# A fused attention and MLP kernel on one core: new load order, new order of the first MLP units, casts moved between engines, last output product by token block

## The chip, the core and the metric

The kernel runs on one core of one Trainium2 chip. The time is the device time of one execution in microseconds (us); the span of the profile is about 1.8 us shorter. PE is the matmul engine (TensorE), PEld its weight load, DVE is VectorE, ACT is ScalarE, POOL is GpSimd, SP is SyncE, which here only issues DMAs. "Granted clock" is the share of full speed that the profile says PE was given. "Unit (c, j)" below means the j-th of the 16 slices of 128 hidden columns of the MLP for chunk c of 512 tokens; there are nine chunks.

## The reference, cut to what matters

```
q_s = softmax(q, axis=-1)                 # 8 batches, 8 heads, 576 tokens, 64 wide
k_s = softmax(k, axis=2)                  # over the tokens
kv  = einsum('bhsd,bhse->bhde', k_s, v)
x   = einsum('bhsd,bhde->bhse', q_s, kv)  # heads joined: 4608 tokens x 512
h   = x @ w_in                            # 512 -> 2048
out = (h * sigmoid(beta * h)) @ w_out     # 2048 -> 512, float32
```

## The kernel before

One chunk is the first 512 tokens of one batch; the ninth chunk collects the 64 left-over tokens of all eight. For each unit the kernel does `mm_a` (four matmuls, then tanh on ACT and a product on DVE, which give `g`), and two units later `mm_b` (four matmuls that add `g` times a slice of `w_out` into four accumulators). In the code cuts NJ is these 16 slices, LAG the two units, HP the four head pairs, and `warm(n)` issues n dummy matmuls whose result nobody reads. All inputs are float32, so weights, `v`, `k` and `q` pass through a cast or an exponential before PE can use them. While chunk c runs, `side` prepares batch c + 1. Chunks 0 and 1 are special, because they run while the weights still arrive. I call the stretch from the end of chunk 0's units to chunk 1's unit 4 the bridge.

The loads and the start of chunk 0:

```python
load_q(0, parts=2)
nc.sync.dma_start(beta_r[:], ...)
load_kv(k_st, k, 0, "k_st", parts=2)
w_load("in", 0, 0)                       # half of the first block of w_in
load_kv(v_st, v, 0, "v_st", parts=4)
w_load("in", 0, 1)
w_load("out", 0); w_load("in", 1); w_load("out", 1); w_load("in", 2)
w_load("out", 2); w_load("in", 3)
load_q(1, parts=2); w_load("out", 3)
load_kv(k_st, k, 1, ...); load_kv(v_st, v, 1, ...)
# ... cut: memsets, identities ...
warm(18)                                 # dummy matmuls
# ... cut: exponential, sum and product of q ...
for s in range(2):
    for j in (2 * s, 2 * s + 1):
        q_pet(0, j, nc.scalar if s == 0 else nc.vector)   # transpose on PE, copy
    warm(10 if s == 0 else 2)
for j in range(HP):
    kz_exp(0, j)                         # two exponentials on ACT each
# ... for each of four head pairs: cast v, kv product, normalise,
#     x product (copied by ACT), mm_a of units 0 and 1, one quarter each
```

Then units 2 to 15 of chunk 0, `mm_a(0, u)` and `mm_b(0, u - 2)` in turn, with the weight casts and the q work of batch 1 between them; the bridge; and the tail:

```python
for s in range(2):
    vz_cast(1, 2 * s, nc.vector, m=2)
for jj in range(2):
    kv_mm(1, jj); kv_norm(1, jj)
mm_b(0, NJ - 2)
for j in range(HP):
    x_mm(1, j, ...)
# ... mm_a of units (1, 0) and (1, 1) ...
finish_b(0, NJ - 1)                      # last mm_b of chunk 0 and its stores
# ... cut: seven equal chunks ...
for st, j in ((0, J0), (0, J1), (1, J0), ...):    # last three units, mixed
    mm_b(B, j, [st])
    if j == J2:
        store(B, st)                     # two stores: blocks 0 to 2, and block 3
```

The softmax here doesn't subtract the row's maximum and nothing guards it: scores larger than these inputs give would overflow.

## Time and profile before

303.77 us median of three runs (302.3 to 303.79); the profiled run is 304.01 us with a span of 302.2 us. The next fence is the windows view of the kernel before, cut at the starts of unit (0, 4), unit (0, 15), unit (1, 4) and of unit 14 of the last chunk. Columns: stretch, its length, busy us and (in brackets) number of instructions of PE, PEld, DVE, ACT and POOL; then granted PE clock, busy share of the DMA engines, GB/s.

```profile
0.00:26.24 26.24, 20.86 (x115) 8.87 (x116) 16.23 (x27) 15.68 (x25) 10.32 (x19) 0.93 0.96 341
26.24:48.64 22.40, 20.38 (x105) 9.52 (x104) 17.38 (x25) 11.66 (x17) 9.75 (x14) 1.00 1.06 371
48.64:63.93 15.29, 12.66 (x81) 6.18 (x80) 9.12 (x18) 7.49 (x12) 2.65 (x3) 0.89 0.45 112
63.93:288.46 224.53, 224.53 (x1153) 105.44 (x1152) 141.66 (x228) 126.72 (x182) 13.38 (x14) 1.00 0.47 134
288.46:302.20 13.74, 5.51 (x25) 2.17 (x23) 3.40 (x5) 2.47 (x5) 0.00 (x0) 0.77 0.31 76
```

Three quarters of the span, the fourth line, is PE busy without a gap at full clock. A change of order can win only in the other four stretches, 78 us in all. In the first two the DMA engines are saturated (0.96 and 1.06).

The timeline of PE, kernel before: start, length, line, what was computed, and in brackets the idle time before it and what ended it.

```profile
26.24 1.03 PE L319 MATMUL h_4_389<-xT_80,w_in_b 128*128 128x512 bf16 x4
...
46.36 0.38 PE L245 MATMUL tp_2_558<-identity,eq_494 128*128 128x128 bf16 x4 [1.72 <-DVE qsT_532 L140]
...
48.64 1.03 PE L319 MATMUL h_15_587<-xT_80,w_in_b 128*128 128x512 bf16 x4
...
53.13 0.92 PE L259 MATMUL kv_0_602<-va_145,ek_143 128*128 128x65 bf16 x18 [2.61 <-DVE va_145 L140]
...
63.93 1.03 PE L319 MATMUL h_4_723<-xT_81,w_in_b 128*128 128x512 bf16 x4
...
293.59 0.38 PE L347 MATMUL acc_3_2720<-w_out_b,g_15_2879 128*128 128x512 bf16 x1
```

PE waits 1.72 us for the copies of transposed q and 2.61 us for the cast of v. Two DVE lines of the same kernel will be compared later: the product that normalises q, and the two casts of v.

```profile
40.88 1.23 DVE L226 TENSOR_TENSOR eq_494<-eq_494,rq_496 128x1024 bf16<-128x1024 bf16 x1
...
52.23 1.43 DVE L140 CAST va_145<-v_st_118 128x1152 bf16<-128x1152 f32 x2
```

The windows view of the kernel before around its two clock drops:

```profile
12.45:15.86 3.41, 1.36 (x21) 0.84 (x21) 1.36 (x6) 3.33 (x7) 1.69 (x3) 1.00 1.07 372
15.86:19.27 3.41, 3.35 (x17) 1.23 (x18) 1.26 (x4) 1.40 (x4) 1.22 (x2) 0.51 1.04 386
50.00:53.41 3.41, 0.80 (x12) 0.34 (x11) 1.78 (x3) 1.57 (x2) 0.00 (x0) 1.00 1.10 279
53.41:56.82 3.41, 3.41 (x38) 2.19 (x35) 1.74 (x7) 0.00 (x0) 1.60 (x1) 0.51 0.20 47
```

After a stretch of 3.41 us in which PE was busy for 1.36 or 0.80 us, the next 3.41 us run at half clock. (The clock column misses the very start: the first dummy matmuls, up to 5.4 us, start 0.43 us apart, which is half the rate of the 0.216 us seen later.) The last view of the kernel before is SP's queue at the end, where the second line is the store that lands last:

```profile
294.24 1.34 SPq L370 DMA_DIRECT2D out_dram<-o_0_2889  x2
295.68 1.29 SPq L370 DMA_DIRECT2D out_dram<-o_3_2899  x1
```

### The profile page before, as it was taken

The page shows a single profiled execution, that of the slowest core. Times are in us where ns is not written, and L with a number is a line of the kernel's source. Part 1 is how long each engine was busy: PE and PEld are TensorE (multiplying, and loading weights), DVE is VectorE, ACT ScalarE, POOL GpSimd, SP SyncE. Part 2 cuts the span into 40 slices and gives each one's busy share as a digit, 9 for nine tenths or more (in the row PEclk, how much of TensorE's full clock was granted, in tenths as well). Part 3 has the DMA queues.
Part 4 walks back from the last instruction along what each step waited for, and adds up shares of the span by engine and source line. Part 5 has one row for each costly group of instructions (what it writes and reads, how often), then busy time and mean ns, then how long its engine had stood idle before and what let it go on. Part 6 is the DMA issues. An engine that isn't in the chain of part 4 may idle for free.

```text
span 302.2 us, 3897 instructions
## 1 busy us (share of the span) xinstructions
PE 283.9 (94%) x1475; PEld 132.2 (44%) x1475; DVE 187.8 (62%) x302; ACT 164.0 (54%) x237; POOL 36.1 (12%) x49
## 2 busy tenths in 40 slices
PE   8689985999999999999999999999999999999990
PEld 2334432544544444444445444544454444544430
DVE  7636885478649654965595559546954694453440
ACT  4854376277459445944594459355835653544440
POOL 4243820300012003000300030003000000000000
PEclk9979999799999999999999999999999999999995
DMA  7999999130973591369037903790396023021005
GB/s 236 380 387 384 372 378 295 40 139 22 316 184 139 160 317 45 141 181 327 16 141 197 317 8 139 222 297 7 135 136 74 30 112 69 0 94 47 0 0 139
DMA packets 55841, 50.05 MB, mean 166 GB/s; under 512 B 26112, under 2 KB 47632, under 8 KB 55824
## 3 DMA queue, kind: packets, MB, share of 16 engines
q1 hardware_dynamic: 55744, 49.69, 54.5%
q8 instruction: 11, 0.18, 0.2%
q10 hardware_dynamic: 80, 0.13, 0.1%
q14 instruction: 6, 0.05, 0.0%
HBM read 36.71 MB, written 9.44 MB: 153 GB/s over the span
## 4 chain that ended last, share of the span: by engine, by line
PE 87%; ACT 4%; DVE 4%; DMA 1%; issue 1%; ACTq 0%; DVEq 0%
ACT ek_138 L153 2%; DMA q_st_83<-in_q_dram 1%; PE acc_0_2717 L347 1%; PE acc_3_2720 L347 1%; PE acc_3_714 L347 1%; PE acc_0_2156 L347 1%; PE acc_0_1578 L347 1%; PE acc_3_1581 L347 1%; PE acc_0_1000 L347 1%; PE acc_2_2448 L347 1%; PE acc_2_1869 L347 1%; PE acc_0_1867 L347 1%; PE acc_2_1002 L347 1%; PE acc_0_711 L347 1%; PE acc_1_2718 L347 1%; PE acc_3_2449 L347 1%
## 5 line engine op out<-in xcount | busy, mean ns | idle before, releaser
L319 PEld LDWEIGHTS <-w_in_b 128*128 128x128 bf16 x576 | 55.5, 98 | 65.5 <-issue 3.1
L389 PEld LDWEIGHTS <-kvp 128*128 128x128 bf16 x34 | 3.7, 115 | 5.9 <-issue 3.2
L140 POOL CAST va_1036<-v_st_826 128x2048 bf16<-128x2048 f32 x1 | 1.9, 1917 | 32.0 <-DMA v_st_826<-in_v_dram 32.0
L299 PEld LDWEIGHTS <-kvp 128*128 128x128 bf16 x32 | 3.3, 102 | 5.4 <-ACT kvp L292 1.8
L153 ACT ACTIVATE ek_138<-k_st_87 64x576 bf16<-64x576 f32 x8 | 5.5, 681 | 0.1
L140 POOL CAST va_2192<-v_st_1997 128x2048 bf16<-128x2048 f32 x1 | 1.9, 1919 | 27.7 <-DMA v_st_1997<-in_v_dram 27.7
L140 POOL CAST va_1903<-v_st_1708 128x2048 bf16<-128x2048 f32 x1 | 1.9, 1919 | 27.6 <-DMA v_st_1708<-in_v_dram 27.6
L140 POOL CAST va_1614<-v_st_1419 128x2048 bf16<-128x2048 f32 x1 | 1.9, 1922 | 27.1 <-DMA v_st_1419<-in_v_dram 27.1
L153 ACT ACTIVATE ek_143<-k_st_115 64x1152 bf16<-64x1152 f32 x4 | 4.6, 1154 | 0.0
L140 POOL CAST va_1325<-v_st_1130 128x2048 bf16<-128x2048 f32 x1 | 1.9, 1919 | 22.3 <-DMA v_st_1130<-in_v_dram 22.3
L209 ACT ACTIVATE eq_183<-q_st_83 128x1024 bf16<-128x1024 f32 x2 | 2.1, 1056 | 3.0 <-DMA q_st_83<-in_q_dram 3.0
L140 POOL CAST va_773<-v_st_126 128x2048 bf16<-128x2048 f32 x1 | 1.9, 1920 | 14.6 <-DMA v_st_126<-in_v_dram 14.6
L138 ACT CAST xT_81<-x_0_652 128x512 bf16<-128x512 f32 x1 | 0.6, 585 | 5.5 <-PE x_0_652 L299 5.5
L259 PE MATMUL kv_0_602<-va_145,ek_143 128*128 128x65 bf16 x18 | 0.9, 214 | 2.6 <-DVE va_145 L140 2.6
L259 PEld LDWEIGHTS <-ek_138 128*128 128x128 bf16 x36 | 1.9, 109 | 3.3 <-issue 2.3
L140 POOL CAST w_in_b<-w_in_90 128x1024 bf16<-128x1024 f32 x2 | 2.1, 1038 | 10.2 <-DMA w_in_90<-in_moe_w_in_dram 10.2
L259 PEld LDWEIGHTS <-ek_143 128*128 128x128 bf16 x36 | 1.8, 122 | 3.1 <-issue 3.1
L140 POOL CAST w_out_b<-w_out_102 128x1024 bf16<-128x1024 f32 x2 | 2.6, 1340 | 3.4 <-DMA w_out_102<-in_moe_w_out_dram 3.4
L140 POOL CAST w_out_b<-w_out_106 128x1024 bf16<-128x1024 f32 x2 | 2.5, 1268 | 2.8 <-DMA w_out_106<-in_moe_w_out_dram 2.8
L220 DVE TENSOR_REDUCE rq_496<-eq_494 128x16 f32<-128x1024 bf16 x2 | 2.4, 1218 | 0.3 <-ACT eq_494 L209 0.3
L220 DVE TENSOR_REDUCE rq_738<-eq_736 128x16 f32<-128x1024 bf16 x2 | 2.4, 1212 | 0.3 <-ACT eq_736 L209 0.3
L220 DVE TENSOR_REDUCE rq_1010<-eq_1008 128x16 f32<-128x1024 bf16 x2 | 2.4, 1192 | 0.3 <-ACT eq_1008 L209 0.3
(1477 smaller groups left out, 853.6 us busy)
## 6 DMA issues: line engine op xcount, KB each, us to landing
k_st_87<-in_k_dram SPq DMA_DIRECT2D x2, 576.0 KB, 7.0
v_st_92<-in_v_dram SPq DMA_DIRECT2D x4, 288.0 KB, 8.9
k_st_115<-in_k_dram SPq DMA_DIRECT2D x2, 576.0 KB, 10.8
v_st_118<-in_v_dram SPq DMA_DIRECT2D x2, 576.0 KB, 11.3
q_st_83<-in_q_dram SPq DMA_DIRECT2D x2, 512.0 KB, 4.3
w_in_90<-in_moe_w_in_dram SPq DMA_DIRECT2D x2, 512.0 KB, 9.2
w_out_98<-in_moe_w_out_dram SPq DMA_DIRECT2D x1, 1024.0 KB, 10.2
w_in_100<-in_moe_w_in_dram SPq DMA_DIRECT2D x1, 1024.0 KB, 11.4
```

The costliest lines, as they stand in the source:

```text
L138: eng.copy(dst, src)
L140: eng.tensor_copy(dst, src)
L153: nc.scalar.activation(ek[b][r, j : j + m, :, e * D : (e + 1) * D], k_st[b][r, j : j + m, :].rearrange("p j (i d) -> p j i d", i=RW), ACTF ...
L209: nc.scalar.activation(eq[b][:, :, s * m : (s + 1) * m, :].rearrange("p i h d -> p h i d"), q_st[b][:, s * m : (s + 1) * m, :].rearrange(" ...
L220: nc.vector.tensor_reduce(rq[b][:, 0, :, h], eq[b][:, :, h, :], axis=AX.X, op=ALU.add)
L259: nc.tensor.matmul(t[:, jl, 0:D1], ek[b][:, j, i, :], va[b][:, j, i, :], start=(i == 0), stop=(i == RW - 1),)
L299: nc.tensor.matmul(t[:], kvp[:, c, j, :], qsT[c][:, :, j, :])
L319: nc.tensor.matmul(h[:], w_in_b[:, kt, ds(j * P, P)], x_of(c)[:, kt, :], start=(kt == 0), stop=(kt == KT - 1),)
L347: nc.tensor.matmul(acc[st][:], g[:, ds(st * P, P)], w_out_b[:, j, :], start=(j == 0), stop=(j == NJ - 1),)
L389: nc.tensor.matmul(t[:, 0:cols], kvp[:, B - 1, 0, :], kvp[:, B - 1, :, :].rearrange("p j r -> p (j r)")[:, 0:cols],)
```

## The change

The intent: feed attention first (k and v ahead of the weights, weights in halves, so that each half is usable when it lands); put four `mm_a` ahead of the first `mm_b`, so that PE has work while tanh and DVE produce the first `g`; spread the weight casts and batch 1's q work so that PE does not wait; use the last output product of chunk 0 to cover the v cast; and finish the output by token block so that half of it leaves early. Cut to its core (the split of chunk 0's v casts over the two engines and fewer dummy matmuls between its kv products are left out):

```diff
+    load_kv(k_st, k, 0, "k_st", parts=4)
+    load_kv(v_st, v, 0, "v_st", parts=4)
     nc.sync.dma_start(beta_r[:], ...)
-    load_kv(k_st, k, 0, "k_st", parts=2)
-    w_load("in", 0, 0)
-    load_kv(v_st, v, 0, "v_st", parts=4)
-    w_load("in", 0, 1)
-    w_load("out", 0)                       # ... and five more whole blocks
+    for blk in range(3):
+        for kind in ("in", "out"):
+            for half in range(2):
+                w_load(kind, blk, half)
     load_q(1, parts=2)
+    w_load("in", 3, 0)
+    w_load("in", 3, 1)
+    w_load("out", 3, 0)                    # ... k of batch 1, out 3 half 1, v
@@ kv_norm: both halves on VectorE
-            if n == 1 and e == 1:
-                nc.scalar.mul(dst[:, 0, :], src[:, 0, :], rk[r, 0, :])
@@ start
-            q_pet(0, j, nc.scalar if s == 0 else nc.vector)
+            q_pet(0, j, nc.vector)
@@ first units
+    w_cast("in", 1, 0, nc.vector)
+    mm_a(0, 2)
+    mm_a(0, 3)
+    w_cast("in", 1, 1, nc.vector)
+    mm_b(0, 0)
+    mm_b(0, 1)
+    for kind, blk in (("out", 1), ("in", 2), ("out", 2), ("in", 3), ("out", 3)):
+        for half in range(2):
+            w_cast(kind, blk, half, nc.gpsimd)      # "in" was on VectorE
+    # ... then the memsets of vt and ekt on GpSimd, now behind all these casts
+    # (before: behind those of "out" 2, ahead of block 3)
+    for u in range(4, NJ):
+        mm_a(0, u); mm_b(0, u - LAG)
+        # q_exp, q_sum at u = 10, 12; q_mul at 11, 13; q_pet at 12 (ScalarE)
+        # and 14 (VectorE); kz_exp from 13. Before: q work at 10 and 11,
+        # q_pet at 12 and 13, kz_exp at 13 and 14
@@ bridge
+    mm_b(0, NJ - 2)
+    # vz_cast of batch 1, VectorE
+    finish_b(0, NJ - 1)                    # now ahead of kv
+    # kv_mm, kv_norm, warm(4), kv_mm, kv_norm; x_mm; units (1, 0) to (1, 3)
@@ tail
-            lo, hi = (0, 3) if st < 3 else (3, 4)
+            lo, hi = ((0, 2), (0, 2), (2, 3), (3, 4))[st]
+    last = [(0, j) for j in range(NJ - 4, NJ - 1)] + [(1, j) for j in range(NJ - 4, NJ - 1)]
+    last += [(0, NJ - 1), (1, NJ - 1)] + [(st, j) for st in (2, 3) for j in range(NJ - 4, NJ)]
```

More of the change, by code (lines that the diff above doesn't have):

```diff
@@ L290, in kv_norm @@
             src = t[r, :, 0:D] if b < NW else t[r, :, e * D1 : e * D1 + D]
-            if n == 1 and e == 1:
-                nc.scalar.mul(dst[:, 0, :], src[:, 0, :], rk[r, 0, :])
-            else:
-                nc.vector.tensor_tensor(dst, src, rk[r].to_broadcast((D, n, D)), ALU.mult)
+            nc.vector.tensor_tensor(dst, src, rk[r].to_broadcast((D, n, D)), ALU.mult)
     def x_mm(c, j, eng, tag="att"):
@@ L310, with mm_a @@
     h_of = {}
-    def mm_a(c, j, kts=None):
+    def mm_a(c, j, kts=None, tag=None):
         kts = range(KT) if kts is None else kts
         if (c, j) not in h_of:
-            tag = "att" if c < NW and j == LAG else "h"
+            tag = tag or ("att" if c < NW and j in (2, 3) else "h")
             h_of[c, j] = ps.tile([P, MAIN], F32, tag=tag, bufs=2, name=f"h{c}_{j}")
@@ L395 @@
     load_q(0, parts=2)
+    load_kv(k_st, k, 0, "k_st", parts=4)
+    load_kv(v_st, v, 0, "v_st", parts=4)
     nc.sync.dma_start(beta_r[:], moe_beta.rearrange("(j p) -> j p", p=P))
-    load_kv(k_st, k, 0, "k_st", parts=2)
-    w_load("in", 0, 0)
-    load_kv(v_st, v, 0, "v_st", parts=4)
-    w_load("in", 0, 1)
-    w_load("out", 0)
-    w_load("in", 1)
-    w_load("out", 1)
-    w_load("in", 2)
-    w_load("out", 2)
-    w_load("in", 3)
-    load_q(1, parts=2)
-    w_load("out", 3)
-    load_kv(k_st, k, 1, "k_st", parts=2)
+    for blk in range(3):
+        for kind in ("in", "out"):
+            for half in range(2):
+                w_load(kind, blk, half)
+    load_q(1, parts=2)
+    w_load("in", 3, 0)
+    w_load("in", 3, 1)
+    w_load("out", 3, 0)
+    load_kv(k_st, k, 1, "k_st", parts=4)
+    w_load("out", 3, 1)
     load_kv(v_st, v, 1, "v_st", parts=2)
@@ L422, with load_next, finish_b @@
     v_buf(1)
+    def load_next(nb):
+        if nb < B:
+            load_q(nb)
+            load_kv(k_st, k, nb, "k_st")
+            load_kv(v_st, v, nb, "v_st")
+        elif nb == B:
+            load_qtail()
+    def finish_b(c, j):
+        mm_b(c, j)
+        if j == NJ - 1:
+            for st in range(R):
+                store(c, st)
     warm(18)
@@ L434 @@
         kz_exp(0, j)
-    w_cast("in", 0, 0, nc.gpsimd)
     tb = ps.tile([P, 512], F32, tag="h", bufs=2, name="tb")
-    nc.tensor.transpose(tb[:, 0:NJ], beta_r[:], ident16[:])
-    nc.vector.tensor_copy(beta_t[:], tb[:, 0:NJ])
     def attn0(p):
         if 0 < p < 3:
-            warm(2, tag="acc3")
-        vz_cast(0, p, nc.gpsimd if p in (0, 1) else nc.vector)
-        if p == 1:
-            w_cast("in", 0, 1, nc.gpsimd)
+            warm(1, tag="acc3")
+        if p % 2 == 0:
+            vz_cast(0, p, nc.gpsimd)
+            vz_cast(0, p + 1, nc.vector)
         kv_mm(0, p, n=1, tag=f"acc{p}")
@@ L451 @@
         attn0(p)
+        if p == 2:
+            w_cast("in", 0, 0, nc.gpsimd)
         if p >= 1:
             x_mm(0, p - 1, nc.scalar)
+        if p == 1:
+            nc.tensor.transpose(tb[:, 0:NJ], beta_r[:], ident16[:])
+            nc.vector.tensor_copy(beta_t[:], tb[:, 0:NJ])
         if p >= 2:
@@ L457 @@
     x_mm(0, HP - 1, nc.scalar)
+    for kind, blk in (("in", 0), ("out", 0)):
+        for half in range(2):
+            if (kind, half) != ("in", 0):
+                w_cast(kind, blk, half, nc.gpsimd)
     for kt in (2, 3):
@@ L460 @@
             mm_a(0, j, [kt])
-    def side0(u):
-        if u == 0:
-            w_cast("out", 0, 0, nc.gpsimd)
-            w_cast("out", 0, 1, nc.gpsimd)
-        if u in (1, 2):
-            w_cast("in", 1, u - 1, nc.vector)
-        if u == 3:
-            w_cast("out", 1, 0, nc.gpsimd)
-            w_cast("out", 1, 1, nc.gpsimd)
-        if u in (5, 6):
-            w_cast("in", 2, u - 5, nc.vector)
-        if u == 7:
-            w_cast("out", 2, 0, nc.gpsimd)
-            w_cast("out", 2, 1, nc.gpsimd)
-            for t in range(2):
-                nc.gpsimd.memset(vt[t][:], 0.0)
-                nc.gpsimd.memset(ekt[t][:], 0.0)
-                for e in range(2):
-                    nc.gpsimd.memset(vt[t][ds(e * TAIL, TAIL), e, :, D:D1], 2.0)
-        if u in (8, 9):
-            w_cast("in", 3, u - 8, nc.vector)
-        if u in (10, 11):
-            q_exp(1, u - 10)
-            q_sum(1, u - 10)
-            q_mul(1, u - 10)
-        if u == 11:
-            w_cast("out", 3, 0, nc.gpsimd)
-            w_cast("out", 3, 1, nc.gpsimd)
-        if u in (12, 13):
-            for j in (2 * (u - 12), 2 * (u - 12) + 1):
-                q_pet(1, j, nc.vector)
-        if u in (13, 14):
-            kz_exp(1, 2 * (u - 13), m=2)
@@ new lines @@
+    w_cast("in", 1, 0, nc.vector)
[5 more added lines that the diff above has]
+    for kind, blk in (("out", 1), ("in", 2), ("out", 2), ("in", 3), ("out", 3)):
+        for half in range(2):
+            w_cast(kind, blk, half, nc.gpsimd)
+    for t in range(2):
+        nc.gpsimd.memset(vt[t][:], 0.0)
+        nc.gpsimd.memset(ekt[t][:], 0.0)
+        for e in range(2):
+            nc.gpsimd.memset(vt[t][ds(e * TAIL, TAIL), e, :, D:D1], 2.0)
@@ new lines @@
+    for u in range(4, NJ):
+        mm_a(0, u)
+        mm_b(0, u - LAG)
+        if u in (10, 12):
+            q_exp(1, (u - 10) // 2)
+            q_sum(1, (u - 10) // 2)
+        if u in (11, 13):
+            q_mul(1, (u - 11) // 2)
+        if u in (12, 14):
+            for j in (u - 12, u - 11):
+                q_pet(1, j, nc.scalar if u == 12 else nc.vector)
+        if u >= 13:
+            kz_exp(1, u - 13)
+    kz_exp(1, 3)
+    mm_b(0, NJ - 2)
+    for s in range(2):
+        vz_cast(1, 2 * s, nc.vector, m=2)
@@ L496, in side @@
+    finish_b(0, NJ - 1)
+    for jj in range(2):
+        kv_mm(1, jj)
+        kv_norm(1, jj)
+        if jj == 0:
+            warm(4)
+    for j in range(HP):
+        x_mm(1, j, nc.scalar if j % 2 == 0 else nc.vector, tag="h" if j < 2 else "att")
+    for kt in range(KT):
+        for j in range(2):
+            mm_a(1, j, [kt])
+    mm_a(1, 2)
+    mm_a(1, 3)
+    mm_b(1, 0)
+    mm_b(1, 1)
     def side(c, u):
@@ L524, in side @@
             load_next(c + 2)
-    def load_next(nb):
-        if nb < B:
-            load_q(nb)
-            load_kv(k_st, k, nb, "k_st")
-            load_kv(v_st, v, nb, "v_st")
-        elif nb == B:
-            load_qtail()
-    def finish_b(c, j):
-        mm_b(c, j)
-        if j == NJ - 1:
-            for st in range(R):
-                store(c, st)
-    side0(0)
-    side0(1)
-    for u in range(2, NJ):
-        mm_a(0, u)
-        mm_b(0, u - LAG)
-        side0(u)
-    for s in range(2):
-        vz_cast(1, 2 * s, nc.vector, m=2)
@@ L548 @@
-    for jj in range(2):
-        kv_mm(1, jj)
-        kv_norm(1, jj)
-    mm_b(0, NJ - 2)
-    for j in range(HP):
-        x_mm(1, j, nc.scalar if j % 2 == 0 else nc.vector, tag="h" if j < 2 else "att")
-    for kt in range(KT):
-        for j in range(2):
-            mm_a(1, j, [kt])
-    finish_b(0, NJ - 1)
-    seq = []
-    for c in range(1, NCH):
-        for j in range(NJ):
-            if (c, j) not in ((1, 0), (1, 1)):
-                seq.append(("A", c, j))
-            if c == 1 and j < LAG:
-                continue
-            bc, bj = (c, j - LAG) if j >= LAG else (c - 1, NJ + j - LAG)
-            if (c, j) == (B, NJ - 1):
-                continue
-            seq.append(("B", bc, bj))
-            seq.append(("S", c, j))
@@ L571 @@
-    order = []
-    skip = set()
-    for n, it in enumerate(seq):
-        if n in skip:
-            continue
-        kind, c, j = it
-        if kind == "B" and j == 0:
-            nxt = next(m for m in range(n + 1, len(seq)) if seq[m][0] == "A")
-            order.append(seq[nxt])
-            skip.add(nxt)
-        order.append(it)
-    side(1, 0)
-    side(1, 1)
-    for kind, c, j in order:
-        if kind == "A":
-            mm_a(c, j)
-        elif kind == "B":
-            finish_b(c, j)
-        else:
-            side(c, j)
@@ L591 @@
-    J0, J1, J2 = NJ - 3, NJ - 2, NJ - 1
-    for st, j in (
-        (0, J0), (0, J1), (1, J0), (1, J1), (2, J0), (2, J1), (3, J0),
-        (0, J2), (1, J2), (2, J2), (3, J1), (3, J2),
-    ):
-        mm_b(B, j, [st])
-        if j == J2:
+    for u in range(4):
+        side(1, u)
+    for c in range(1, NCH):
+        for j in range(4 if c == 1 else 0, NJ - 1 if c == B else NJ):
+            lead = c > 1 and j == 3
+            if not lead:
+                mm_a(c, j)
+            if c > 1 and j == 2:
+                mm_a(c, 3)
+            if (c, j) == (B, NJ - 2):
+                pass
+            elif j >= LAG:
+                mm_b(c, j - LAG)
+            else:
+                finish_b(c - 1, NJ + j - LAG)
+            side(c, j)
@@ L598 @@
+    mm_a(B, NJ - 1, tag="att")
+    last = [(0, j) for j in range(NJ - 4, NJ - 1)] + [(1, j) for j in range(NJ - 4, NJ - 1)]
+    last += [(0, NJ - 1), (1, NJ - 1)] + [(st, j) for st in (2, 3) for j in range(NJ - 4, NJ)]
+    for st, j in last:
+        mm_b(B, j, [st])
+        if j == NJ - 1:
             store(B, st)
```

## The prediction

> **What bounds the kernel now.** The page gives TensorE (PE) 94% of the 302.2 us span. From 64 to 290 us the windows view shows PE busy all the time at full clock (matmul starts 0.216 us apart), and one chunk repeats every 29.8 us (timeline: first unit at 86.8, next chunk's at 116.6). The order listing shows the same instruction order there after the change, so nothing can be won there. Room exists only at the two ends.
>
> Before, on the PE timeline:
> - Start: the first two MLP units finish at 22.2, unit 4 starts at 26.24 us. The chain of waits runs through eight ScalarE exponentials (9.9 to 15.5 us), then kv, normalise, x, copy, four times. DMA is saturated meanwhile: landing times fit 4.5 us + bytes / 0.379 MB per us (k 10.4, first weights 16.3, next 19.0 and 21.8 us).
> - First chunk's end: PE idles 0.3, 1.7 and 2.6 us (waits: on VectorE's q work, then on the v cast), and the clock halves from 53 to 57 us (matmul spacing 0.43). Unit 15 ends at 49.5, the next chunk's unit 4 starts at 63.93.
> - Tail: last matmul starts 293.6; its store is issued at 295.7 behind a 768 KB one and lands 300.8.
>
> **What the change does, costed with these durations.**
> 1. k, v first: v lands at 11.2 to 13.5 instead of 12.6 to 15.3 us; the exponentials (0.68 us each) need not wait for the two qsT copies, now on VectorE, and end near 13.5. The first weights half lands later (11.8 becomes 14.9), its GpSimd cast (1.04 us) ends near 16, and PE's order puts kv of pair 3 behind it: a new wait, which limits the gain. Units 0 and 1 should finish near 19.1 instead of 22.2.
> 2. Units 2 and 3 ahead of the first output product fill the tanh/VectorE latency (a 0.42 us wait). The next weights half (landing 20.4) is cast in time. Unit 4 starts near 22.5: gain 3.7 us, estimate.
> 3. The q work of chunk 1 is spread over more units: PE waits of 2.0 us fall to about 0.7. Further weight halves go through GpSimd (ten of 1.04 to 1.5 us over about 19 us) and should stay ahead of PE; DMA (third block in near 35, v of chunk 1 near 44) is then almost as late as PE needs it. Unit 15 ends near 44: gain 5.5 us so far.
> 4. The last output product now fills the v-cast wait, and there is no clock drop; from unit 15's end to the next chunk's unit 4 the estimate is 11.6 us instead of 14.4. Gain 8.3 us in total, carried unchanged through the steady stage.
> 5. Tail: half the output leaves earlier, but one more pair of issues (0.67 us each) stands in the queue, and PE ends 0.2 us later. Gain about 1 us.
>
> Sum 9.3 us; I take off 0.8 for a clock drop in the start. The Trainium skill ("TensorE: Matmul & The Clock Gate", Part 1) says that an idle window of about 3.4 us halves the clock; this trace agrees (drops from 16.0 to 19.3 and 53.4 to 56.8).
>
> **Prediction:** 295.2 us, range 292.5 to 298.8. Faster by over 2% 0.79, within 2% 0.20, slower 0.01.
>
> **Right or wrong if:** unit (0,4) starts near 22.5 and (1,4) near 55.6 us; no half clock between 45 and 60 us; steady chunk still 29.8 us; last landing within 6 us of the last matmul.
>
> **What would make it wrong:** GpSimd casts falling behind (locking with VectorE), DMA delivering the third weights block, k or v of chunk 1 late so that ScalarE's in-order queue blocks tanh, or a clock drop in either bridge.

## The result, and the profile after

295.31 us median (295.13 to 295.51, four runs) against 303.78 us (302.3 to 304.08, four runs). The ratio is 0.9731 with a 95% interval of 0.9699 to 0.9763. A ratio here is always the mean time of one kernel's fast runs over that of the other's of the same rounds, so it is not quite the ratio of the medians.

The windows view of the changed kernel, cut at the same events:

```profile
0.00:21.88 21.88, 18.56 (x111) 8.51 (x114) 17.13 (x33) 13.72 (x19) 9.31 (x17) 1.00 0.95 330
21.88:43.51 21.63, 20.28 (x104) 9.29 (x104) 13.71 (x19) 12.24 (x18) 11.15 (x10) 1.00 1.07 372
43.51:56.75 13.24, 12.03 (x86) 5.72 (x85) 10.44 (x20) 8.85 (x15) 4.97 (x11) 1.00 1.09 325
56.75:281.28 224.53, 223.31 (x1130) 105.54 (x1152) 141.50 (x227) 126.71 (x182) 15.80 (x17) 1.00 0.47 131
281.28:293.50 12.22, 5.52 (x25) 2.09 (x23) 3.45 (x5) 2.57 (x5) 0.00 (x0) 0.95 0.32 86
```

The long stretch has the same 224.53 us to the hundredth (some matmul records are missing there, so its busy time is not the place to look). The clock column is 1.00 in the three stretches at the front, where before it was 0.93, 1.00 and 0.89. By subtraction of the two fences:

| stretch | before | after | gain | predicted gain |
|---|---|---|---|---|
| to unit (0, 4) | 26.24 | 21.88 | 4.36 | 3.7, less 0.8 held back for a clock drop |
| to unit (0, 15) | 22.40 | 21.63 | 0.77 | 1.8 |
| bridge, to unit (1, 4) | 15.29 | 13.24 | 2.05 | 2.8 |
| to the last chunk's unit 14 | 224.53 | 224.53 | 0 | 0 |
| tail | 13.74 | 12.22 | 1.52 | 1.0 |
| sum | 302.20 | 293.50 | 8.70 | 8.5 |

The sum was right because two terms were too large (by 1.0 and 0.75 us) and two too small (by 0.7 us, or 1.5 with the 0.8 held back, and by 0.5): that the total fell within 0.1 us of the forecast is partly luck. The PE timeline of the changed kernel shows where the two smaller gains went:

```profile
21.88 1.03 PE L316 MATMUL h_4_412<-xT_80,w_in_b 128*128 128x512 bf16 x4
...
35.48 0.38 PE L344 MATMUL acc_3_385<-w_out_b,g_9_484 128*128 128x512 bf16 x1
36.21 1.04 PE L316 MATMUL h_12_522<-xT_80,w_in_b 128*128 128x512 bf16 x4 [0.35 <-DVE rq_505 L220]
...
38.87 0.38 PE L245 MATMUL tp_0_539<-identity,eq_503 128*128 128x128 bf16 x4 [0.76 <-DVE eq_503 L226]
...
43.51 1.03 PE L316 MATMUL h_15_594<-xT_80,w_in_b 128*128 128x512 bf16 x4
...
47.76 0.74 PE L259 MATMUL kv_0_628<-va_156,ek_154 128*128 128x65 bf16 x18 [0.63 <-DVE va_156 L140]
...
56.75 1.03 PE L316 MATMUL h_4_742<-xT_81,w_in_b 128*128 128x512 bf16 x4
...
286.63 0.38 PE L344 MATMUL acc_3_2739<-w_out_b,g_15_2894 128*128 128x512 bf16 x1
```

Matmuls start 0.216 us apart at full clock, so unit 12 could have started at 35.48 + 0.22 = 35.70 us. The view names DVE's q reduction as what ended that wait. Unit 12 needs no result of that reduction. The timeline of DVE (first two lines below) and of POOL (the rest) in the changed kernel tells more:

```profile
36.94 1.78 DVE L226 TENSOR_TENSOR eq_503<-eq_503,rq_505 128x1024 bf16<-128x1024 bf16 x1
...
45.90 2.40 DVE L140 CAST va_156<-v_st_129 128x1152 bf16<-128x1152 f32 x2
```

```profile
35.11 1.04 POOL L140 CAST w_in_b<-w_in_118 128x1024 bf16<-128x1024 f32 x1 [3.47 <-DMA w_in_118<-in_moe_w_in_dram]
...
36.61 1.04 POOL L140 CAST w_in_b<-w_in_118 128x1024 bf16<-128x1024 f32 x1 [0.46 <-DMA w_in_118<-in_moe_w_in_dram]
37.97 1.65 POOL L140 CAST w_out_b<-w_out_121 128x1024 bf16<-128x1024 f32 x1 [0.33 <-DMA w_out_121<-in_moe_w_out_dram]
...
43.76 0.96 POOL L487 MEMSET vt_75<- 128x1040 bf16 x1
...
45.50 0.97 POOL L487 MEMSET vt_76<- 128x1040 bf16 x1
46.40 0.53 POOL L488 MEMSET ekt_78<- 128x512 bf16 x1
46.87 0.82 POOL L490 MEMSET vt_76<- 64x8 bf16 x2
```

The first half of the fourth block of input weights lands at 35.1 us, and its cast ends at 36.15, just ahead of unit 12. The q product takes 1.78 us where it took 1.23 before. It begins at 36.94, while a POOL cast (36.61, its usual 1.04 us) is running; the next POOL cast begins at 37.97, while the product is running, and takes 1.65 us. Later the second q product begins first (41.70 us) and keeps its usual 1.22 us, and the POOL cast that begins beside it (42.34) takes 1.48. So each fits being held up by what began before it. The two v casts take 2.40 us where they took 1.43 before, beside POOL's memsets, which before ran from 32.3 us, away from any v cast; nearly all of it falls on the first of the two (1.72 us, the second 0.77).

SP's queue at the end, changed kernel; from the start of the last matmul to the end of the span it is now 6.87 us (293.50 - 286.63) instead of 8.61 us:

```profile
286.07 1.34 SPq L367 DMA_DIRECT2D out_dram<-o_0_2903  x2
287.51 1.65 SPq L367 DMA_DIRECT2D out_dram<-o_2_2913  x2
289.25 0.71 SPq L367 DMA_DIRECT2D out_dram<-o_3_2921  x1
```

### The profile page after: what moved, and what is told of

Its sections match the earlier page's. It is cut to its first block, busy times and chain, and to the rows that moved or that the text cites. A ratio compares the mean times of both kernels' runs of the same rounds, so it can differ in the third digit from the quotient of the medians.

```text
span 293.5 us, 3886 instructions
## 1 busy us (share of the span) xinstructions
PE 279.7 (95%) x1449; PEld 131.1 (45%) x1477; DVE 186.2 (63%) x302; ACT 164.1 (56%) x237; POOL 41.2 (14%) x53
## 4 chain that ended last, share of the span: by engine, by line
PE 86%; DVE 7%; ACT 2%; DMA 1%; issue 1%; DVEq 0%; ACTq 0%
DMA q_st_83<-in_q_dram 1%; PE acc_1_731 L344 1%; PE acc_0_2465 L344 1%; PE acc_2_2467 L344 1%; PE acc_0_1019 L344 1%; PE acc_1_2737 L344 1%; PE acc_3_2468 L344 1%; PE acc_2_1021 L344 1%; PE acc_3_733 L344 1%; PE acc_1_2176 L344 1%; PE acc_0_2175 L344 1%; PE acc_0_1886 L344 1%; PE acc_2_1599 L344 1%; PE acc_1_1598 L344 1%; PE acc_0_1308 L344 1%
## 5 line engine op out<-in xcount | busy, mean ns | idle before, releaser
L153 ACT ACTIVATE ek_149<-k_st_86 64x576 bf16<-64x576 f32 x8 | 5.5, 682 | 0.3 <-DVE rq_196 L221 0.2
L153 ACT ACTIVATE ek_154<-k_st_123 64x576 bf16<-64x576 f32 x8 | 5.4, 677 | 0.1
L140 POOL CAST va_1055<-v_st_845 128x2048 bf16<-128x2048 f32 x1 | 1.9, 1918 | 22.5 <-DMA v_st_845<-in_v_dram 22.5
L226 DVE TENSOR_TENSOR eq_503<-eq_503,rq_505 128x1024 bf16<-128x1024 bf16 x2 | 3.0, 1498 | 0.0
L140 POOL CAST va_152<-v_st_91 128x576 bf16<-128x576 f32 x2 | 1.9, 950 | 6.8 <-DMA v_st_91<-in_v_dram 6.8
L220 DVE TENSOR_REDUCE rq_196<-eq_194 128x16 f32<-128x1024 bf16 x2 | 2.4, 1216 | 0.3 <-ACT eq_194 L209 0.3
L220 DVE TENSOR_REDUCE rq_505<-eq_503 128x16 f32<-128x1024 bf16 x2 | 2.4, 1214 | 0.3 <-ACT eq_503 L209 0.3
L220 DVE TENSOR_REDUCE rq_757<-eq_755 128x16 f32<-128x1024 bf16 x2 | 2.4, 1212 | 0.3 <-ACT eq_755 L209 0.3
L220 DVE TENSOR_REDUCE rq_1318<-eq_1316 128x16 f32<-128x1024 bf16 x2 | 2.4, 1192 | 0.3 <-ACT eq_1316 L209 0.3
L220 DVE TENSOR_REDUCE rq_1607<-eq_1605 128x16 f32<-128x1024 bf16 x2 | 2.4, 1192 | 0.3 <-ACT eq_1605 L209 0.3
```

Of the source, the lines that this page charges most:

```text
L140: eng.tensor_copy(dst, src)
L153: nc.scalar.activation(ek[b][r, j : j + m, :, e * D : (e + 1) * D], k_st[b][r, j : j + m, :].rearrange("p j (i d) -> p j i d", i=RW), ACTF ...
L220: nc.vector.tensor_reduce(rq[b][:, 0, :, h], eq[b][:, :, h, :], axis=AX.X, op=ALU.add)
L226: nc.vector.tensor_tensor(eq[b][:, :, h, :], eq[b][:, :, h, :], rq[b][:, 1, :, h].unsqueeze(3).to_broadcast((P, R, m, D)), ALU.mult,)
```

## The experiments

My theory was that the gain is a sum of separate pieces, each carried unchanged through the PE-bound stretch. The rivals: the gain is mainly the two clock drops that the change happens to avoid; one part, the lead of four units or the load order, makes it; or pieces hide behind each other, so that they do not add. Every run gave a correct result. The changed kernel was not run again in the experiments, and not all of them ran on the same chip, so differences of about 0.3 us from it are not told from none; the starts of units in the profiles tell more. Medians are compared with 295.31 us for the changed kernel and, within one call, with the kernel before (303.82 us, 303.30 us, 303.64 us and 303.02 us in the four calls).

### 1. The tail alone (b_tail)

The kernel before, with only the tail part of the diff above, and the last unit's `mm_a` put next to the one before it.

> The kernel before with the new tail alone (last two MLP units together, output product by token block, three stores). My theory, that the gain is a sum of four independent pieces: the last unit-14 start to the end of the span shrinks from 13.7 to about 12.2 us, everything ahead stays, so 1.5 us faster (ratio near 0.995). Rival, that the tail gains nothing by itself because the store queue only gets one more pair of issues: no difference.

302.58 us against 303.82 us, ratio 0.9953 (0.9921 to 0.9985). From the start of unit 14 of the last chunk to the end it is 12.45 us (288.45 to 300.9) instead of 13.74. The tail is worth some 1.3 us by itself; this piece does add. The other traces agree: from unit 14 to the end the old tail takes 13.74 and 13.75 us (two traces), the new one 11.9 to 12.5 us (twelve).

### 2. Dummy matmuls against the clock drops (b_warm)

```diff
+        if p == 0:
+            warm(6, tag="acc3")        # ahead of the first kv product
@@ bridge
+    warm(12, tag="att")                # ahead of kv of chunk 1
```

> The kernel before with dummy matmuls filled into its two long PE gaps (6 before the first kv product, 12 before chunk 1's kv product) and nothing else. Rival theory, that most of the gain is the two halved-clock stretches which the change happens to avoid: 3 us or more faster. My theory, that the order of the work makes most of it: the start is bound by the chain of exponentials, kv and copies and gains at most 0.8 us, the bridge gains about 1.5 us from full clock; about 2 us faster together, 6 us or more still missing.

302.32 us against 303.82 us, ratio 0.9957 (0.9927 to 0.9986). The windows view of this run, the same stretches as for the kernel before:

```profile
12.45:15.86 3.41, 3.07 (x24) 1.17 (x23) 0.54 (x3) 3.09 (x6) 1.87 (x3) 1.00 1.07 373
15.86:19.27 3.41, 2.60 (x33) 1.21 (x29) 2.09 (x6) 1.95 (x5) 1.04 (x1) 1.00 1.05 386
50.00:53.41 3.41, 3.40 (x20) 1.39 (x18) 1.62 (x3) 1.73 (x2) 0.00 (x0) 1.00 1.08 287
53.41:56.82 3.41, 3.38 (x46) 2.01 (x45) 2.69 (x9) 1.00 (x2) 0.28 (x1) 1.00 0.23 60
```

Both drops are gone (1.00 where it was 0.51). Unit (0, 4) starts at 25.98 instead of 26.24 us and unit (1, 4) at 62.61 instead of 63.93. The bridge alone (unit 15 at 48.80 to unit (1, 4)) takes 13.81 instead of 15.29 us, 1.48 less, while 0.42 us were lost on the way to it. So the clock is worth about 1.5 us of the 8.5, nearly all of it in the bridge, and the rival falls as the main cause. But of the bridge's own gain of 2.05 us it is the larger part. The run explains something else too. The kernel before spreads over 3 us from run to run, and its span goes, loosely, with the mean granted clock: in the runs of this call the span was 300.6 to 301.0 us at 0.995, 301.9 to 302.2 at 0.984 to 0.986 and 303.9 at 0.974, but 301.2 in one run at 0.978. The version with the dummy matmuls had spans of 300.4 to 301.2 in all six runs. Drops that come in one run and not in another would explain most of the spread; only one run of this kernel left a trace, so this is not shown.

### 3. A lead of two units, not four (a_lead2)

```diff
     mm_a(0, 2)
-    mm_a(0, 3)
     w_cast("in", 1, 1, nc.vector)
     mm_b(0, 0)
+    mm_a(0, 3)
     mm_b(0, 1)
```

> The changed kernel with only two, not four, MLP units ahead of the first output product. My theory: the lead is the small part, it covers one wait for tanh and the product with it: unit 4 starts 0.4 to 0.7 us later, total plus 0.5 us. Rival, that the lead is what makes the start gain of 4.4 us: plus 2 us or more.

295.40 us: no difference. The PE timeline of this run:

```profile
19.80 1.04 PE L344 MATMUL acc<-w_out_b,g 128*128 128x512 bf16 x4 [0.42 <-DVE g L328]
...
36.22 1.03 PE L316 MATMUL h<-xT,w_in_b 128*128 128x512 bf16 x4
```

The wait of 0.42 us for the first `g` is back, and unit 4 starts at 22.41 instead of 21.88 us, as expected. But unit 12 starts at 36.22, and in the changed kernel at 36.21. There the weights were late anyway. The lead saves half a microsecond and the kernel then waits half a microsecond; my expected plus 0.5 us in total was wrong. The run shows one thing more: its q product begins later (37.46 us, when POOL's cast is over) and takes only 1.21 us, and the transposes behind it still wait 0.71 us.

### 4. The old order of the first loads (a_oldhead)

```diff
+    nc.sync.dma_start(beta_r[:], ...)
+    load_kv(k_st, k, 0, "k_st", parts=2)
+    w_load("in", 0, 0)
+    load_kv(v_st, v, 0, "v_st", parts=4)
+    w_load("in", 0, 1)              # all else as in the changed kernel
```

> The changed kernel with the old order of the first loads (beta and the halves of the first weights mixed between k and v). My theory: v arrives 1.5 to 2.2 us later, so the kv products and everything behind them in the start do too; unit 4 starts 1.0 to 2.0 us later, total plus 1 to 2 us. Rival, that the order of the loads does not matter because the first weights half bounds the start anyway: no more than 0.3 us.

295.53 us median; four of the six runs took 295.47 to 295.56 and two 296.48 and 296.59. The profile is of the slowest: unit 4 starts at 22.89 us, 1.0 later as expected, and unit 12 at 37.38, because in that run the fourth weights block landed 1.2 us later too (its cast begins at 36.28). There the loads were late from early on (the first cast of output weights begins at 18.00 us, and at 17.04 in the changed kernel), so how much of the 1.0 us is the order and how much that slow run is not shown. The other four runs left no trace; whether they lost as much at the start and caught up, or lost less, is open. With the old order the kernel was 0.2 us slower in most runs and 1.2 us in some.

### 5. The old engines in the start (a_oldeng)

The first two q copies and the second half of each normalisation go back to ScalarE, as in the kernel before.

> The changed kernel with the old choice of engines in the start (first two q transposes copied by ScalarE, second half of each normalisation on ScalarE). My theory: the two copies stand ahead of the eight exponentials on ScalarE and the half normalisations behind them, so the kv products come later: unit 4 starts about 1 us later, total plus 1 us. Rival, that VectorE is now the tighter engine in the start (it is busy without a pause from 11 to 17 us) and giving work back to ScalarE helps or does nothing: 0 to minus 0.5 us.

296.05 us. Unit 4 starts at 23.97 us, 2.1 later; unit 12 1.6 later (37.78); unit (1, 4) only 0.55 later (57.30). The choice of engines is the largest part of the start's gain that these runs find, and again most of it is given back further on: in this run the wait of 0.63 us ahead of chunk 1's kv product is gone, because the v casts come after POOL's memsets (they start at 47.41 us and take 1.42 us together).

### 6. The old bridge (a_oldbridge)

kv and x of chunk 1 and its units 0 and 1 ahead of `finish_b(0, NJ - 1)` again, and no `warm(4)`. (`mm_b(0, NJ - 2)` stays ahead of the v casts, where the change put it: the old bridge is not restored in full.)

> The changed kernel with the old bridge between chunk 0 and 1 (kv of chunk 1 ahead of the last output product of chunk 0, no dummy matmuls). My theory: the last output product no longer fills the wait for the v cast; PE waits about 1.5 us longer there and may drop its clock; total plus 1 to 2.5 us. Rival, that the bridge is set by VectorE's casts and normalisations whatever PE does meanwhile: within 0.3 us.

295.39 us median (294.97, 295.28, 295.51 and 296.71). The rival was right for three of the four runs: the bridge is set by DVE's casts and normalisations, whatever PE does meanwhile. The profile is of the slow run, and its windows view shows the stretch ahead of a drop:

```profile
46.24:49.65 3.41, 1.71 (x38) 1.40 (x38) 3.10 (x6) 1.80 (x3) 2.28 (x5) 1.00 1.11 340
```

PE was busy 1.71 us of 3.41, the clock then halved for 3.4 us, and unit (1, 4) started at 58.19 us instead of 56.75. PE waits 1.50 us for the v cast there and not 0.63, yet the kv product starts at 47.91 us, hardly later than 47.76: the cast sets it. What the new bridge buys in these runs is protection from that drop, not the covering of a wait; whether the order or the four dummy matmuls give the protection was not tested apart.

### 7. The memsets out of the bridge (a_memset)

```diff
     v_buf(1)
+    for t in range(2):
+        nc.gpsimd.memset(vt[t][:], 0.0)     # and the others; GpSimd idles here
```

> The changed kernel with the GpSimd memsets of the tail buffers (4 us) moved from the bridge to the start, where GpSimd idles from 4 to 10 us. My theory: they slow VectorE's two v casts of chunk 1 from 0.71 to 1.2 us each (2.40 against 1.43 us in the kernel before); without them the casts take about 1.4 us again, chunk 1's kv product starts about 0.6 us earlier, total minus 0.6 to 1.0 us. Rival, that the slow casts are not on the chain, or are slow for another reason: no difference.

294.20 us (294.12 to 294.27), 1.1 us faster than the changed kernel. The DVE timeline of this run:

```profile
45.79 1.42 DVE L140 CAST va<-v_st 128x1152 bf16<-128x1152 f32 x2
```

The two casts take 1.42 us again instead of 2.40. Chunk 1's kv product starts at 46.85 instead of 47.76 us without a wait, unit (1, 4) at 55.67 instead of 56.75. This shows that the memsets had slowed the casts and that the casts were on the chain.

### 8. The fourth weights block ahead of q of chunk 1 (a_in3first)

```diff
+    w_load("in", 3, 0)
     load_q(1, parts=2)
-    w_load("in", 3, 0)
     w_load("in", 3, 1)
```

> The changed kernel with the first half of the fourth block of input weights loaded ahead of q of chunk 1, not behind. My theory: it lands about 2.7 us earlier, unit 12 no longer waits for its cast and starts at 35.7 instead of 36.2 us; total minus 0.3 to 0.5 us, less if q then comes late. Rival, that unit 12 waited for VectorE's q reduction as the list of waits says: no difference.

295.29 us (295.04 to 295.88): no difference. The PE timeline of this run, of the slowest of the four:

```profile
35.66 1.03 PE L316 MATMUL h<-xT,w_in_b 128*128 128x512 bf16 x4
...
39.44 0.61 PE L245 MATMUL tp<-identity,eq 128*128 128x128 bf16 x8 [1.89 <-DVE eq L226]
```

Unit 12 starts at 35.66 us without a wait, so it had waited for the weights and not for the q reduction that the profile named. But q is later now, DVE's q product runs beside POOL's casts (2.09 us), and the transposes wait 1.89 us instead of 0.76. One wait was traded for another.

### 9. A better start alone (a_startx)

All v casts of chunk 0 on GpSimd, and all kv and x products ahead of the first `mm_a`.

> The changed kernel with its start improved alone: all four v casts of chunk 0 on GpSimd, and the four kv and x products ahead of the first MLP products. My theory after the runs so far: unit 4 starts 0.8 to 1.2 us earlier, but unit 12 then still waits for the cast of the fourth block of input weights, which lands when it did (cast from 35.1 to 36.2 us), so the rest of the kernel starts when it did: total within 0.3 us. Rival, that what is won in the start is kept to the end as in the prediction's sum: minus 0.8 to 1.2 us.

295.04 us (294.75 to 295.47). The first half of my expectation missed: unit 4 starts only 0.18 us earlier (21.70), since PE now begins its first `mm_a` at 16.5 us, not at 15.3, and runs them without a gap. Unit 12 starts at 36.22 us all the same, behind a wait of 0.55 us for POOL's weight cast. The test of what becomes of a gain there is therefore a small one; it agrees with the lead of two.

### 10. Early memsets, and one more last store on ScalarE's queue (d1)

```diff
-                    (nc.scalar if e and st == 3 else nc.sync).dma_start(
+                    (nc.scalar if e and st >= 2 else nc.sync).dma_start(
```

> The changed kernel with the early memsets and with ScalarE's queue issuing two of the five last stores (one more than now). Memsets were measured at minus 1.1 us. Tail: three stores, not four after the first pair, stand in SyncE's queue, so the last one is issued about 0.7 us earlier and the end comes 0.5 to 0.9 us earlier; total minus 1.6 to 2.0 us against the changed kernel. Rival for the tail, that the last landing is set by the data and not by the queue: minus 1.1 us only.

294.25 us, no better than with the early memsets alone (294.20). From unit 14 to the end it is 12.0 us against 12.2, and the traces of the same tail without this edit spread from 11.9 to 12.5. The tail's rival was right in that fewer issues in the queue bring nothing measurable.

### 11. All of it (d2)

d1 with the better start, the fourth weights block first, and chunk 1's q transposes at units 13 and 14 on VectorE.

> d1 with the improved start, the first half of the fourth weights block loaded ahead of q of chunk 1, and chunk 1's first q transposes one unit later and on VectorE. My theory: only together do they help, as each wait hid behind the next: unit 12 starts near 35 us and the transposes no longer wait, so another 0.5 to 1.3 us under d1; v of chunk 1, which lands near 45 us, is the limit. Rival, that the saturated DMA up to 45 us bounds the bridge and nothing ahead of it matters: within 0.3 us of d1.

294.24 us: nothing over d1. The PE timeline of this run:

```profile
37.18 1.03 PE L316 MATMUL h<-xT,w_in_b 128*128 128x512 bf16 x4
...
43.05 0.71 PE L245 MATMUL tp<-identity,eq 128*128 128x128 bf16 x8 [1.54 <-DVE qsT L140]
```

The first line is unit 13 (unit 12 started at 35.46). The second pair of transposes then waits 1.54 us for DVE, whose in-order queue has the copies of the first pair behind another q product. Everything won up to unit 13 was lost there.

### 12. The same with the q work placed anew (d3)

Early memsets, the better start, the fourth weights block first; and

```diff
-        if u in (12, 14):
-            for j in (u - 12, u - 11):
-                q_pet(1, j, nc.scalar if u == 12 else nc.vector)
-        if u >= 13:
-            kz_exp(1, u - 13)
+        if u in (13, 15):
+            for j in (u - 13, u - 12):
+                q_pet(1, j, nc.scalar if u == 13 else nc.vector)
+        if u >= 14:
+            kz_exp(1, u - 14)              # q_pet ahead of q_mul of that unit
```

> The changed kernel with the early memsets, the improved start, the fourth weights block half ahead of q of chunk 1, and a new place for chunk 1's transposes (units 13 on ScalarE and 15 on VectorE) and k exponentials (from unit 14). My theory from the last runs: in each trial one wait hid behind another (late weights, then VectorE's q work, then the v casts); with all three out of the way unit 15 starts near 41 to 42 us instead of 43.4, and the v of chunk 1 (landing near 45 us) and VectorE set the bridge: 0.5 to 1.2 us under the version with early memsets alone (294.2 us). Rival, that VectorE's in-order queue from 35 to 50 us is already full and bounds the bridge: within 0.3 us of it.

293.16 us (292.89 to 293.40), ratio to the kernel before 0.9672 (0.9647 to 0.9697): it beats the changed kernel by 2.1 us and the version with early memsets by 1.0 (another chip; the traces agree, unit (1, 4) starts at 54.70 and 55.67 us). The PE timeline of this run, then its DVE timeline:

```profile
41.49 1.02 PE L316 MATMUL h<-xT,w_in_b 128*128 128x512 bf16 x4
...
45.46 0.74 PE L259 MATMUL kv<-va,ek 128*128 128x65 bf16 x18
```

```profile
45.48 0.76 DVE L140 CAST va<-v_st 128x1152 bf16<-128x1152 f32 x1 [0.17 <-DMA v_st<-in_v_dram]
```

Unit 15 starts at 41.49 us, two us earlier than in the changed kernel (in part because the second pair of transposes now stands behind it), and the kv product follows the last output product without a wait, at 45.46 instead of 46.85 us with early memsets alone. The second v cast now waits 0.17 us for its data, as expected; that the loads are the next limit of the whole bridge is not shown.

## Why the prediction was right or wrong, point by point

- **The total (295.2 us predicted, 295.31 measured), and that the long stretch changes nothing: right.** The stretch kept its 224.53 us. That step carried the prediction: once it holds, only four short stretches have to be costed. Of the checks set beforehand, a steady chunk of 29.8 us (29.78), no half clock between 45 and 60 us and the last landing within 6 us of the last matmul (292.20 less 286.63, 5.57 us) held; unit (1, 4) came 1.1 us late, at 56.75 instead of 55.6, and the 0.8 us held back and the tail made up for it.
- **Start (unit 4 near 22.5 us, measured 21.88): right in mechanism, 0.6 us too cautious.** Loads landed up to 0.8 us ahead of my fit (first weights half 14.1 us where I had 14.9). The further 0.8 us that I took off for a clock drop was not needed: between 12.45 and 15.86 us PE is busy 2.83 us in the changed kernel. Experiments 3 to 5 share out the start at unit 4: engines 2.1, lead 0.5 and load order at most some 1.0 us (from one slow run), up to 3.6 of the 4.36.
- **"PE waits of 2.0 us fall to about 0.7": the step that was mis-sized.** The stretch gained 0.77 us, not 1.8. Unit 12 waited 0.5 us for weights that landed late, and the transposes 0.76 us for a q product that had grown from 1.23 to 1.78 us. The growth is not the whole of that wait: in experiments 3 and 5 the product took 1.21 us, began later, and the transposes still waited 0.71 us. I had used durations from a trace in which POOL was quiet at that moment, and wrote the casts locking with VectorE only as a risk. I had also written "third block in near 35"; it was the fourth, and it was not almost but just too late.
- **"From unit 15's end to the next chunk's unit 4 the estimate is 11.6 us": mis-sized, 12.38 measured** (56.75 less the end of unit 15's matmuls at 44.37). The term is the v casts, 2.40 us and not 1.43, and experiment 7 shows their cause.
- **"The last output product now fills the v-cast wait, and there is no clock drop": half right.** There was no drop. But undoing most of this order, with its dummy matmuls, cost nothing in three of four runs (experiment 6); its worth there is the protected clock, which is 1.48 of the 2.05 us that the bridge gained (experiment 2).
- **Tail (about 1 us): measured 1.52 in the profiles, 1.2 in the medians of experiment 1.** The mechanism was as stated; PE did end 0.2 us later (5.35 against 5.13 us from unit 14 to the last matmul).
- **That the pieces add: shown only for the tail.** Undone one at a time, the lead costs 0.1, the load order 0.2, the engines 0.7 and the bridge 0.1 us in the medians, 1.1 us together. With the tail (1.3) that is far from 8.5. Of these only the 0.7 is clear of the 0.3 us that tell nothing. In the traces of experiments 3, 5 and 9, what a part lost or won at unit 4 was gone, whole or in part, by unit 12 or unit (1, 4), in a wait that came anyway. The clock (1.5 us) lies across the parts.
- **Open:** the spreading of the weight casts and of batch 1's q work was not undone by itself, nor were two parts undone together, so how the remaining gain, more than half of the 8.5 us, divides between them is not settled. Nor is why two of six runs of experiment 4 were 1 us slower.

Two statements of the Trainium skill bear on this. "TensorE: Matmul & The Clock Gate", Part 1, says that the clock halves after at least one idle window of about 3.4 us; the traces agree on the length (3.41 us at half clock) but the window need not be idle: drops followed stretches of 3.41 us with PE busy for 0.80, 1.36 and, in one run, 1.71 us. "SBUF — State Buffer", "SBUF: two separate sides", says that GpSimd shares a port pair with VectorE, which needs it in its two-port modes, or when it has two inputs in SBUF and the GpSimd instruction reads SBUF; whichever starts first holds the pair for its whole instruction, and the other is blocked. The traces agree in kind: q product (two inputs in SBUF) 1.23 to 1.78 us beside a POOL cast, v casts 1.43 to 2.40 us beside memsets, and 1.42 again without them. In which mode a v cast runs no trace shows.

## What to carry to other kernels

Cost an operation with its duration in the company that it will have after the change: a cast or memset put on GpSimd is not free where it runs beside VectorE work that is on the chain; moving 4 us of memsets away from it gave 1.1 us here. Where loads saturate the DMA engines, as in this kernel up to 45 us, gains need not add: after each step ask which wait comes next, and take the waits out together (experiments 8, 9 and 11 took out some and gave 0.3 us or less, experiment 12 took out the three waits found and gave 1 us more). A wait put down to an engine whose result the instruction does not need was something else, here a load and its cast (experiment 8).

## What the Trainium skill lacked or had wrong

- "TensorE: Matmul & The Clock Gate", Part 1: it speaks of an idle window and names no share of busy time. Here stretches of 3.41 us with PE busy for 0.80, 1.36 and 1.71 us were followed by half clock, while one with 1.69 us (43.17 to 46.58 us of the kernel before) was not. So the busy time of the view alone does not draw the limit, and no page read for this gives it.
- "SBUF — State Buffer", "SBUF: two separate sides", gives the lock but no cost for these pairs: two float32 to bf16 VectorE casts beside GpSimd memsets took 2.40 instead of 1.43 us, a bf16 product of two SBUF inputs beside a GpSimd cast 1.78 to 2.09 instead of 1.23 us, and the GpSimd cast 1.65 instead of 1.04 us.
